# A decode step of attention with a gate: the last heads' output as columns, turned into 16 rows of 32

## The chip, the cores and the metric

The kernel runs on one core of a Trainium2 chip. Its time is device microseconds of one execution. The core has five engines that run side by side: TensorE (PE; the loading of its weights is shown as PEld), VectorE (DVE), ScalarE (ACT), GpSimd (POOL) and SyncE (SP), which here only issues DMAs. Data lie in HBM, in SBUF (128 partitions) and in PSUM, where TensorE writes its products. Engines wait for one another and for DMAs through semaphores.

## What is computed

One token x (512 numbers) is normalised to xn. Attention runs over the last 4096 positions of a cache of 32 heads with 128 numbers a head, and its result is multiplied by wo. A small MLP on xn gives a gate g, and the output is x + s * g.

```python
xn = _layernorm(x)
q = (xn @ wq)                       # 32 heads of 128
scores = q . k[:, last 4096, :] * 128**-0.5
o = softmax(scores) . v[:, last 4096, :]
s = o.reshape(4096) @ wo            # 4096 x 512
x1 = xn + hs                        # hs is made of shifted h: with one token all of it is zero
g = silu(x1 + gelu(layernorm(x1) @ w3) @ w4)
out = x + s * g                     # 512 numbers, bf16
```

K and V of the window are 32 MB each; with the weights the kernel reads 78.84 MB.

## The kernel before

**Groups.** The heads are taken in 8 groups of G = 4. One K tile or V tile (4 MB) holds a group: the 128 partitions are 4 heads by 32 blocks of 128 positions. The loop runs over s = 0 to 9: in turn s it loads K of group s and V of group h = s - 2 (LAG = 2), makes the scores of group s, the softmax of group s - 1, and the V products of group h. There are three K buffers and two V buffers; the V buffers lie where the front's weights (the pool `wts`) lay. All large loads are issued on SP's queue through `load`, in program order.

**Scores.** Of a group's 128 columns of K, `k_vector` has VectorE multiply some (`nd`: 76, 80 or 64) with q (L343) and sum the products (L345), in four parts a group. The others are turned by TensorE (`k_turn`, L361), copied to SBUF by ScalarE (L364) and multiplied by q on TensorE (`k_scores`, L372). `sm_own`, `sm_max`, `sm_turn`, `sm_exp`, `sm_den` and `sm_rden` are the softmax.

**V.** `v_wide` (L449) multiplies p with V, four columns at once, into four groups of rows of `ov`; ScalarE copies that, `v_turn` (L466) turns it, `v_add` (L471) sums it. In the last group V comes in four pieces (columns 0 to 64, 96, 112, 128); the last two pieces go through `v_part` (L482), whose weights are 128x128 of V and which multiplies four columns of p. `v_out` adds the two results (`both`, L494) and scales them (`o`, L497).

**Output product.** The first 28 heads are multiplied with wo in blocks of 16, 8 and 4 heads (`ox_spread`, `ox_pick`, `y_wide`) into four rows of 512 (`yr_ps`), copied to `y_sum` (L668). The last four heads (`y_head`) use four rows of wo_rows, of which the last (head 31) is loaded by itself, as the last load. `rows_add` (L150) is the helper that the change removes: it takes one column as weights (one column of the array) and multiplies it with a 128x512 matrix in four pieces of 128, so that the result lies as four rows of 128 on the partitions 0, 32, 64 and 96:

```python
for j in range(KC):
    nc.tensor.matmul(ps[32 * j:32 * j + 1, :], lhsT=col, rhs=w[0:k, j * P:(j + 1) * P], ...)
```

`y_ps` is opened with zeros by `rows_open`, gets the rows of `y_sum` (with the indicator `ind` as the column) and those of the last four heads, and is then multiplied by `g_row` (L680), added to `x_row` (L682) and stored from the four partitions.

**The front.** x is loaded as 16 rows of 32 (`x_in`) and turned into a column form for the normalisation. For the end it is also opened into the row form (`r_slot`, `r_row`, `r_up`, `r_in`, `xr_ps`, `x_row`, `xn_row`). The MLP's last sums come as rows `hr` (L295), which `rows_add` adds up into `h2_ps`; `bv` (L300) adds `xn_row`, and `g_row` is its Silu (L302), for which ScalarE loads a table of functions first.

**Order.** Before the loop, a scheduler of the language orders each engine's instructions. In the loop TensorE, VectorE and ScalarE keep the order of the text (`manual_schedule`); what belongs to the front and is not done by then is threaded in by the scheduler. Each engine runs its list in order, so an instruction that waits holds up all behind it.

Of the kernel before, what the change touches and what calls it, by code (L numbers as in the profile page):

```python
# [8 lines left out]
P = 128  # L9
BF16 = mybir.dt.bfloat16  # L10
# [16 lines left out]
def kernel(  # L27
# [43 lines left out]
    small.tile([P, 208], BF16, name="pad")  # L71
    wts_guard = tc.tile_pool(name="wts", bufs=1)
    wts = wts_guard.__enter__()

# [71 lines left out]
    def rows_open(ps):  # L146
        nc.tensor.matmul(ps[:], lhsT=zero_bf[:], rhs=ident_bf[:], start=True, stop=False,
                         skip_group_check=True)

    def rows_add(ps, col, w, last):  # L150
        k = col.shape[0]
        for j in range(KC):
            nc.tensor.matmul(ps[32 * j:32 * j + 1, :], lhsT=col, rhs=w[0:k, j * P:(j + 1) * P],  # L153
                             start=False, stop=last, skip_group_check=True)

    def ln_stats(src_f, tag):
        ps = ps_misc.tile([P, KC], FP32, tag="misc", name="ln_ps")
# [81 lines left out]
    for j in range(KC):  # L239
        for c in range(KC):  # L240
# [9 lines left out]
    nc.vector.tensor_reduce(out=r_slot[:], in_=ident_bf[0:XR, 0:XR].rearrange("k (j a) -> k a j", a=KC), axis=AX.X, op=ALU.max)  # L250
    r_row = wts.tile([XR, KC], BF16, name="r_row")
    nc.vector.tensor_reduce(out=r_row[:], in_=ident_bf[0:XR, 0:XR].rearrange("k (j a) -> k j a", a=KC), axis=AX.X, op=ALU.max)
    r_up = wts.tile([XR, KC, PB], BF16, name="r_up")
    nc.vector.tensor_copy(out=r_up[:], in_=r_row[:].unsqueeze(2).to_broadcast([XR, KC, PB]))
# [3 lines left out]
    xr_ps = ps_misc.tile([P, P], FP32, tag="misc", name="xr_ps")  # L258
# [37 lines left out]
    h2_ps = ps_misc.tile([P, P], FP32, tag="misc", name="h2_ps")  # L296
# [14 lines left out]
    y_ps = ps_y.tile([P, P], FP32, name="y_ps")  # L311
    rows_open(y_ps)

# [119 lines left out]
    def wo_row(h):  # L433
        return wo_rows[:, h - h_part, :]
# [77 lines left out]
    def ox_pick(i, fill=0):  # L512
# [12 lines left out]
                                    op=ALU.add)  # L525
        ox_blk[i] = ox

    y_sum = small.tile([P, D], FP32, name="y_sum")

    yr = {}  # L530

# [27 lines left out]
    for s in range(NG + LAG):  # L559
# [22 lines left out]
        if s < NG:  # L582
            nb = len(batches(s))

            def keys(b0, b1):
                for b in range(b0, b1):
                    k_turn(s, kn, b)
                    if b > 0:
                        k_scores(s, b - 1)

            k_open(s)
            k_vector(s, kn, 0)
            keys(0, 2)
            if s == 7:
                v_turn(h - 1)
                v_add(h - 1)
                v_out(h - 1)
            elif s > 1:
                sm_den(s - 2)
                sm_rden(s - 2)  # L600
            elif s == 1:
                sm_max(0)
            k_vector(s, kn, 1)
            keys(2, 4)
            if s == 7:
                sm_den(h)
                sm_rden(h)
                keys(4, nb - 2)
                sm_turn(s - 1)
                keys(nb - 2, nb)  # L610
            else:
                if s > 0:
                    sm_turn(s - 1)
                keys(4, nb)
            k_scores(s, nb - 1)
            sm_own(s)
            if s == 7:
                k_vector(s, kn, 2)
                v_wide(h, v)
                sm_exp(s - 1)  # L620
                v_turn(h)
                y_open()
                k_vector(s, kn, 3)
                v_add(h)
                v_out(h)
                ox_spread(1)
                sm_max(s)
                continue
            if s > 0:
# [12 lines left out]
            if s == 6:  # L642
                ox_pick(0)
            if s > 0:
                sm_max(s)
        elif s == NG:
            ox_pick(1)
            sm_turn(NG - 1)
            sm_exp(NG - 1)
            y_wide(1, False)  # L650
            sm_den(NG - 2)
            sm_rden(NG - 2)
            y_wide(0, False)
            warm(3)
            v_wide(h, v)
            sm_den(NG - 1)
            sm_rden(NG - 1)
            v_turn(h)
            v_add(h)
            v_out(h)  # L660
            ox_spread(2)
        else:
            v_open(h)
            warm(2)
            v_wide(h, v, cuts[1], last=False)
# [12 lines left out]
    region.__exit__(None, None, None)  # L678
    y = small.tile([P, P], FP32, name="y")
    nc.vector.tensor_tensor(out=y[:], in0=y_ps[:], in1=g_row[:], op=ALU.mult)  # L680
    out_row = small.tile([P, P], BF16, name="out_row")
    nc.vector.tensor_tensor(out=out_row[:], in0=y[:], in1=x_row[:], op=ALU.add)  # L682
    load(out.rearrange("a b (j n) -> (a b j) n", j=KC), out_row[0:P:32, :])


# [28 lines left out]
```

## Time and profile before

| | |
|---|---|
| median of 3 runs | 192.71 us (192.57 to 192.85) |
| profiled execution | 192.51 us |
| its span | 190.7 us |
| VectorE busy | 154.9 us (81%) |
| TensorE busy | 119.6 us (63%), weight loads 74.9 us |
| ScalarE busy | 89.0 us (47%) |
| moved by DMA | 79.02 MB, mean 414 GB/s |
| mean granted TensorE clock | 0.689 of full |

The span is the time from the first instruction to the last that the profiler recorded in one execution. Busy time says how long an engine worked, not whether anything waited for it. In a row of groups or of the timeline stand the line of the kernel, the engine, the operation, `out<-in` by the names of the tiles, their shapes and the count. "Releaser" is what ended an idle time. The strips of digits show 40 equal slices of the span, about 4.8 us each.

### The profile page before, as it was taken

How to read it: one execution, taken by the hardware profiler on the slowest of the kernel's cores; microseconds unless marked ns; L12 is line 12 of the kernel's file. 1: busy time of each engine (PE TensorE's matmuls, PEld its weight loads, DVE VectorE, ACT ScalarE, POOL GpSimd, SP SyncE). 2: the span in 40 equal slices, each digit the busy share in tenths (PEclk: the TensorE clock that was granted, in tenths of full speed). 3: DMA queues.
4: the chain of work that ended last, by engine and by line, in shares of the span. 5: the costliest groups of instructions: out<-in, count | busy, mean ns of one | idle time of the engine just before them, and what ended most of it. 6: DMA issues, size and time to landing. Idle time of an engine off the chain costs nothing.

```text
span 190.7 us, 2819 instructions
## 1 busy us (share of the span) xinstructions
PE 119.6 (63%) x1143; PEld 74.9 (39%) x1143; DVE 154.9 (81%) x184; ACT 89.0 (47%) x191; POOL 2.2 (1%) x10
## 2 busy tenths in 40 slices
PE   2446834778656169436964684573878386769972
PEld 1331313566545154334344433440854075423331
DVE  4830169999999999999999999999999999990112
ACT  2000821978686066607382737362575148644120
POOL 2110000000000000000000000000000000000000
PEclk9999985555555555965585569558575559785897
DMA  5999999999999999999999999999999998999991
GB/s 214 448 404 435 455 402 431 440 440 433 436 435 440 440 440 436 426 433 440 423 412 405 440 436 416 457 440 433 436 440 442 426 419 378 464 426 416 414 380 43
DMA packets 4597, 79.02 MB, mean 414 GB/s; under 512 B 520, under 2 KB 1128, under 8 KB 1640
## 3 DMA queue, kind: packets, MB, share of 16 engines
q1 hardware_dynamic: 4408, 74.65, 91.5%
q10 hardware_dynamic: 176, 4.20, 5.1%
q8 instruction: 9, 0.15, 0.3%
q14 instruction: 4, 0.03, 0.0%
HBM read 78.84 MB, written 0.00 MB: 413 GB/s over the span
## 4 chain that ended last, share of the span: by engine, by line
DVE 71%; DMA 20%; PE 3%; SPq 2%; issue 1%; ACT 1%; DVEq 0%; ACTq 0%
DVE S L345 43%; DVE prod L343 22%; DMA kv<-in_A_k_cache_dram 12%; DMA kv<-in_A_v_cache_dram 8%; SPq L76 2%; PE ov L449 2%; DVE m L388 1%; DVE S L386 1%; ACT kt L364 1%; DVE mx L396 1%; DVE md L398 0%; DVE oT L471 0%; DVE hr L295 0%; DVE ox L524 0%; PE y_ps L153 0%
## 5 line engine op out<-in xcount | busy, mean ns | idle before, releaser
L345 DVE TENSOR_REDUCE S<-prod 128x20 f32<-128x2560 bf16 (+2 forms) x32 | 87.6, 2736 | 1.1
L364 ACT COPY kt<-pt 128x1024 bf16<-128x1024 bf16 (+1 forms) x51 | 49.7, 1004 | 43.9 <-PE pt L361 42.7
L361 PE MATMUL pt<-ident_f,kv 128*128 128x128 f32 x202 | 46.1, 381 | 7.4 <-DMA kv<-in_A_k_cache_dram 7.4
L343 DVE TENSOR_TENSOR prod<-kv,q_bc 128x2560 bf16<-128x2560 bf16 (+2 forms) x32 | 46.1, 1442 | 3.3 <-DMA kv<-in_A_k_cache_dram 3.1
L361 PEld LDWEIGHTS pt<-ident_f,kv 128*128 128x128 f32 x202 | 34.0, 199 | 11.3 <-DMA kv<-in_A_k_cache_dram 8.7
L372 PE MATMUL sT<-q_pair,kt 128*128 128x8 bf16 x404 | 19.0, 170 | 16.2 <-ACT kt L364 16.0
L372 PEld LDWEIGHTS <-kt 128*128 128x128 bf16 x404 | 16.2, 105 | 26.5 <-ACT kt L364 25.5
L449 PE MATMUL ov<-kv,pT 128*16 128x512 bf16 x248 | 24.4, 561 | 0.4 <-DMA kv<-in_A_v_cache_dram 0.4
L394 PE MATMUL mt_ps<-ident_f,m 128*1 128x128 f32 x8 | 2.9, 360 | 18.4 <-DVE rden L421 17.5
L455 ACT COPY ov_sb<-ov 128x512 f32<-128x512 f32 x8 | 4.7, 585 | 20.3 <-PE ov L449 20.3
L410 ACT ACTIVATE pT<-S,mb 128x128 bf16<-128x128 f32 x32 | 14.0, 574 | 0.2
L449 PEld LDWEIGHTS <-pT 128*16 128x16 bf16 x248 | 7.1, 117 | 14.5 <-issue 13.7
L381 ACT ACTIVATE own<-sT,par 128x48 f32<-128x48 f32 (+2 forms) x32 | 7.5, 352 | 3.7 <-PE sT L372 3.7
L466 PE MATMUL ot_ps<-ident_f,ov_sb 128*128 128x128 f32 x32 | 7.5, 378 | 1.8 <-ACT mb L406 1.5
L410 ACT ACTIVATION_READ_ACCUMULATOR pT<-S,mb 128x1 f32 x32 | 8.3, 260 | 0.0
L218 ACT CAST q_row<-qr_ps 128x512 bf16<-128x512 f32 x1 | 0.6, 585 | 16.5 <-PE qr_ps L216 16.5
L394 PEld LDWEIGHTS mt_ps<-ident_f,m 128*1 128x1 f32 x8 | 0.6, 80 | 19.1 <-DVE rden L421 17.9
L403 PE MATMUL mb_ps<-md,par_t 5*128 5x4 f32 x16 | 4.3, 336 | 5.9 <-DVE md L398 5.9
L421 DVE RECIPROCAL rden<-den_ps 128x4 f32<-128x4 f32 x8 | 1.4, 175 | 7.6 <-PE den_ps L416 7.6
L219 DVE CAST q_row<-qr_ps 128x512 bf16<-128x512 f32 x1 | 0.7, 692 | 7.4 <-PE qr_ps L216 7.4
L403 PEld LDWEIGHTS mb_ps<-md,par_t 5*128 5x128 f32 x16 | 3.8, 293 | 6.9 <-PE sT L372 5.6
L466 PEld LDWEIGHTS ot_ps<-ident_f,ov_sb 128*128 128x128 f32 x32 | 4.8, 188 | 2.4 <-ACT mb L406 1.9
(136 smaller groups left out, 85.3 us busy)
## 6 DMA issues: line engine op xcount, KB each, us to landing
kv<-in_A_k_cache_dram SPq DMA_DIRECT2D x7, 4096.0 KB, 30.7
kv<-in_A_v_cache_dram SPq DMA_DIRECT2D x7, 4096.0 KB, 29.6
wq_sb<-in_A_wq_dram ACTq DMA_DIRECT2D x1, 4096.0 KB, 17.3
kv<-in_A_k_cache_dram SPq DMA_DIRECT2D x2, 2048.0 KB, 23.0
wo<-in_A_wo_dram SPq DMA_DIRECT2D x1, 2048.0 KB, 28.8
kv<-in_A_v_cache_dram SPq DMA_DIRECT2D x1, 2048.0 KB, 12.9
w_sb<-in_B_w_dram SPq DMA_DIRECT2D x1, 1376.0 KB, 12.5
w_sb<-in_B_w_dram SPq DMA_DIRECT2D x1, 1280.0 KB, 19.0
```

The source lines that it names most:

```text
L76: return tc.keep_in_program_order(nc.sync.dma_start(out=dst, in_=src))
L343: nc.vector.tensor_tensor(out=prod[:, 0:m, :], in0=kn[:, rows, :], in1=q_bc[:, g:g + 1, :].to_broadcast([P, m, Dh]), op=ALU.mult)
L345: nc.vector.tensor_reduce(out=st[g]["S"][:, rows], in_=prod[:, 0:m, :], axis=AX.X, op=ALU.add)
L361: nc.tensor.transpose(pt[:, i, :], kn[:, c:c + 2, :].rearrange("p c d -> p (c d)").bitcast(FP32), ident_f[:])
L364: nc.scalar.copy(out=kts[b][:, 0:n, :], in_=pt[:, 0:n, :].bitcast(BF16))
L372: nc.tensor.matmul(st[g]["sT"][:, c:c + 2, :].rearrange("p c a -> p (c a)"), lhsT=kt[:, i, l::2], rhs=q_pair[:, g, l, :], start=(l == 0), ...
L381: nc.scalar.mul(s["own"][:, 0:m, a], s["sT"][:, 0:m, a], par[:, a:a + 1])
L403: nc.tensor.matmul(mb_ps[:], lhsT=par_t[:].rearrange("k b a -> k (b a)"), rhs=md[:], start=True, stop=True)
L410: nc.scalar.activation(out=s["pT"][:, :, a], in_=s["S"][:], func=ACT.Exp, scale=scale, bias=mb[:, a:a + 1], accum_out=s["sum"][:, a:a + 1])
L449: nc.tensor.matmul(ov[r:r + 4 * G], lhsT=s["pT"][:, c:c + 4, :].rearrange("p i a -> p (i a)"), rhs=v[:, c:c + 4, :], start=(i < 4), stop=( ...
L455: nc.scalar.copy(out=s["ov_sb"][:], in_=ov[:])
L466: nc.tensor.transpose(ot_ps[:, step * j:step * j + P], s["ov_sb"][:, j, :], ident_f[:])
```

## The change

The last heads' output is made as columns. `y_head` takes 128x128 of wo_rows as weights and multiplies the one column o with it, so that number j * 128 + d of the output lies at partition d, column j, of `y_cols` (part of the tile `yz_ps`). At the end `t_last` multiplies these by `g_own`, the gate with a mask: 16 columns (j, q), in which a partition has its value only where q is its block of 32 partitions. One product with `fold`, which brings together the partitions that are equal modulo 32, makes of it `z_rows`: 16 rows of 32 on the partitions 0 to 15. `x_in` is added and the 16 rows are stored.

The four rows of `y_sum` go the same way: `y_turn` turns them with four transposes, sums the four (`y_first`) and multiplies them by `g_own` (`t_first`); `z_add` adds them into `z_rows` while the last V pieces are still coming. In the front x's normalised form is made as a column (`xn_col`), and the MLP's rows `hr` are summed with `hr` as the weights (128x128, f32) and `ind` as the column, so that `bv` and the gate (`g_col`) are 128x4. Some pads in the pools of tiles are new or of another size.

```diff
-    r_up = wts.tile([XR, KC, PB], BF16, name="r_up")
-    nc.vector.tensor_copy(out=r_up[:], ...)
...
-    nc.tensor.matmul(xr_ps[:], lhsT=r_up[:].rearrange("k j b -> k (j b)"), rhs=r_in[:].rearrange("k a n -> k (a n)"),
-                     start=True, stop=True)
-    x_row = small.tile([P, P], BF16, name="x_row")
-    nc.vector.tensor_copy(out=x_row[:], in_=xr_ps[:])
-    xn_row = small.tile([P, P], FP32, name="xn_row")
-    nc.vector.tensor_scalar(out=xn_row[:], in0=x_row[:], scalar1=negmean[:], scalar2=rstd[:],
+    nc.tensor.matmul(xt_ps[:], lhsT=r_in[:].rearrange("k a n -> k (a n)"), rhs=r_row[:], start=True, stop=True)
+    xn_col = small.tile([P, KC], FP32, name="xn_col")
+    nc.vector.tensor_scalar(out=xn_col[:], in0=xt_ps[:], scalar1=negmean[:], scalar2=rstd[:],
...
-    rows_open(h2_ps)
-    rows_add(h2_ps, ind, hr, True)
-    bv = small.tile([P, P], FP32, name="bv")
-    nc.vector.tensor_tensor(out=bv[:], in0=xn_row[:], in1=h2_ps[:], op=ALU.add)
-    g_row = small.tile([P, P], FP32, name="g_row")
-    nc.scalar.activation(out=g_row[:], in_=bv[:], func=ACT.Silu)
+    for j in range(KC):
+        nc.tensor.matmul(h2_ps[:, j:j + 1], lhsT=hr[:, j * P:(j + 1) * P], rhs=ind[:], start=True, stop=True)
+    bv = small.tile([P, KC], FP32, name="bv")
+    nc.vector.tensor_tensor(out=bv[:], in0=xn_col[:], in1=h2_ps[:], op=ALU.add)
+    g_col = small.tile([P, KC], FP32, name="g_col")
+    nc.scalar.activation(out=g_col[:], in_=bv[:], func=ACT.Silu)
...
+    g_own = small.tile([P, KC, NQ], FP32, name="g_own")
+    nc.vector.tensor_tensor(out=g_own[:], in0=g_col[:].unsqueeze(2).to_broadcast([P, KC, NQ]),
+                            in1=masks[4][2][:].unsqueeze(1).to_broadcast([P, KC, NQ]), op=ALU.mult)
+    fold_f = const.tile([P, XC], FP32, name="fold_f")
+    nc.vector.tensor_reduce(out=fold_f[:], in_=ident_f[:].rearrange("d (i t) -> d t i", t=XC), axis=AX.X, op=ALU.max)
...
-    y_ps = ps_y.tile([P, P], FP32, name="y_ps")
-    rows_open(y_ps)
+    yz_ps = ps_y.tile([P, KC + XC], FP32, name="yz_ps")
...
+    y_cols, z_rows = yz_ps[:, 0:KC], yz_ps[0:XR, KC:KC + XC]
...
     def y_head(h):
-        rows_add(y_ps, o_blk[3][:, h - h_part:h - h_part + 1], wo_row(h), h == H - 1)
+        for j in range(KC):
+            nc.tensor.matmul(y_cols[:, j:j + 1], lhsT=wo_row(h)[:, j * P:(j + 1) * P],
+                             rhs=o_blk[3][:, h - h_part:h - h_part + 1], start=False, stop=(h == H - 1),
+                             skip_group_check=True)
+
+    def y_turn():
+        yt_ps = ps_misc.tile([P, KC, P], FP32, tag="misc", name="yt_ps")
+        for j in range(KC):
+            nc.tensor.transpose(yt_ps[:, j, :], y_sum[:, j * P:(j + 1) * P], ident_f[:])
+        y_first = small.tile([P, KC], FP32, name="y_first")
+        nc.vector.tensor_reduce(out=y_first[:], in_=yt_ps[:].rearrange("p j (i m) -> p j i m", m=32)[:, :, :, 0],
+                                axis=AX.X, op=ALU.add)
+        t_first = small.tile([P, KC, NQ], FP32, name="t_first")
+        nc.vector.tensor_tensor(out=t_first[:], in0=y_first[:].unsqueeze(2).to_broadcast([P, KC, NQ]), in1=g_own[:],
+                                op=ALU.mult)
+        return t_first
+
+    def z_add(t, fold, last):
+        nc.tensor.matmul(z_rows, lhsT=t[:].rearrange("p j q -> p (j q)"), rhs=fold[:], start=False, stop=last,
+                         skip_group_check=True)
...
-            rows_add(y_ps, ind, y_sum, False)
+            t_first = y_turn()
             v_part(h, v, cuts[2], cuts[3])
             v_turn(h)
+            z_add(t_first, fold_f, False)
...
-    y = small.tile([P, P], FP32, name="y")
-    nc.vector.tensor_tensor(out=y[:], in0=y_ps[:], in1=g_row[:], op=ALU.mult)
-    out_row = small.tile([P, P], BF16, name="out_row")
-    nc.vector.tensor_tensor(out=out_row[:], in0=y[:], in1=x_row[:], op=ALU.add)
-    load(out.rearrange("a b (j n) -> (a b j) n", j=KC), out_row[0:P:32, :])
+    t_last = small.tile([P, KC, NQ], BF16, name="t_last")
+    nc.vector.tensor_tensor(out=t_last[:], in0=y_cols.unsqueeze(2).to_broadcast([P, KC, NQ]), in1=g_own[:], op=ALU.mult)
+    z_add(t_last, fold_bf, True)
+    out_sb = small.tile([XR, XC], BF16, name="out_sb")
+    nc.vector.tensor_tensor(out=out_sb[:], in0=z_rows, in1=x_in[:], op=ALU.add)
+    load(out.rearrange("a b (r n) -> (a b r) n", r=XR), out_sb[:])
```

More of the change, by code (lines that the diff above doesn't have):

```diff
@@ L70 @@
     sm_pool = ctx.enter_context(tc.tile_pool(name="sm", bufs=3))
-    small.tile([P, 208], BF16, name="pad")
+    small.tile([P, 240], BF16, name="pad")
     wts_guard = tc.tile_pool(name="wts", bufs=1)
@@ L144, in zeros @@
                          start=True, stop=False, skip_group_check=True)
[L146 to L154, printed above, removed]
     def ln_stats(src_f, tag):
@@ L252 @@
     nc.vector.tensor_reduce(out=r_row[:], in_=ident_bf[0:XR, 0:XR].rearrange("k (j a) -> k j a", a=KC), axis=AX.X, op=ALU.max)
-    r_up = wts.tile([XR, KC, PB], BF16, name="r_up")
-    nc.vector.tensor_copy(out=r_up[:], in_=r_row[:].unsqueeze(2).to_broadcast([XR, KC, PB]))
     r_in = wts.tile([XR, KC, XC], BF16, name="r_in")
@@ L257 @@
                             in1=r_slot[:].unsqueeze(2).to_broadcast([XR, KC, XC]), op=ALU.mult)
-    xr_ps = ps_misc.tile([P, P], FP32, tag="misc", name="xr_ps")
-    nc.tensor.matmul(xr_ps[:], lhsT=r_up[:].rearrange("k j b -> k (j b)"), rhs=r_in[:].rearrange("k a n -> k (a n)"),
-                     start=True, stop=True)
-    x_row = small.tile([P, P], BF16, name="x_row")
-    nc.vector.tensor_copy(out=x_row[:], in_=xr_ps[:])
-    xn_row = small.tile([P, P], FP32, name="xn_row")
-    nc.vector.tensor_scalar(out=xn_row[:], in0=x_row[:], scalar1=negmean[:], scalar2=rstd[:],
+    xt_ps = ps_misc.tile([P, KC], FP32, tag="misc", name="xt_ps")
+    nc.tensor.matmul(xt_ps[:], lhsT=r_in[:].rearrange("k a n -> k (a n)"), rhs=r_row[:], start=True, stop=True)
+    xn_col = small.tile([P, KC], FP32, name="xn_col")
+    nc.vector.tensor_scalar(out=xn_col[:], in0=xt_ps[:], scalar1=negmean[:], scalar2=rstd[:],
                             op0=ALU.add, op1=ALU.mult)
@@ L295 @@
     nc.vector.tensor_copy(out=hr[:], in_=hr_ps[:].rearrange("p j n -> p (j n)"))
-    h2_ps = ps_misc.tile([P, P], FP32, tag="misc", name="h2_ps")
-    rows_open(h2_ps)
-    rows_add(h2_ps, ind, hr, True)
-    bv = small.tile([P, P], FP32, name="bv")
-    nc.vector.tensor_tensor(out=bv[:], in0=xn_row[:], in1=h2_ps[:], op=ALU.add)
-    g_row = small.tile([P, P], FP32, name="g_row")
-    nc.scalar.activation(out=g_row[:], in_=bv[:], func=ACT.Silu)
+    h2_ps = ps_misc.tile([P, KC], FP32, tag="misc", name="h2_ps")
+    for j in range(KC):
[4 more added lines that the diff above has]
+    nc.scalar.activation(out=g_col[:], in_=bv[:], func=ACT.Silu)
     make_masks(16)
@@ L307 @@
     make_masks(4)
-    y_ps = ps_y.tile([P, P], FP32, name="y_ps")
-    rows_open(y_ps)
+    NQ = P // XC
+    g_own = small.tile([P, KC, NQ], FP32, name="g_own")
[3 more added lines that the diff above has]
+    nc.vector.tensor_reduce(out=fold_f[:], in_=ident_f[:].rearrange("d (i t) -> d t i", t=XC), axis=AX.X, op=ALU.max)
+    fold_bf = const.tile([P, XC], BF16, name="fold_bf")
+    nc.vector.tensor_copy(out=fold_bf[:], in_=fold_f[:])
+    yz_ps = ps_y.tile([P, KC + XC], FP32, name="yz_ps")
+    nc.tensor.matmul(yz_ps[:], lhsT=zero_bf[:], rhs=zero_bf[:, 0:KC + XC], start=True, stop=False,
+                     skip_group_check=True)
+    y_cols, z_rows = yz_ps[:, 0:KC], yz_ps[0:XR, KC:KC + XC]
     par = const.tile([P, G], FP32, name="par")
@@ L526, in ox_pick @@
         ox_blk[i] = ox
+    small.tile([P, 48], BF16, name="pad_rows")
     y_sum = small.tile([P, D], FP32, name="y_sum")
+    small.tile([P, 32], BF16, name="pad_result")
     yr = {}
@@ L550, in y_head @@
     def y_head(h):
-        rows_add(y_ps, o_blk[3][:, h - h_part:h - h_part + 1], wo_row(h), h == H - 1)
+        for j in range(KC):
[15 more added lines that the diff above has]
+        nc.tensor.matmul(z_rows, lhsT=t[:].rearrange("p j q -> p (j q)"), rhs=fold[:], start=False, stop=last,
+                         skip_group_check=True)
     NG = H // G
```

## The prediction

> **What bounds the kernel now.** I read the page first: the strip of busy tenths, then the chain that ended last.
>
> ```profile
> span 190.7 us, 2819 instructions
> ...
> DVE  4830169999999999999999999999999999990112
> ...
> DMA  5999999999999999999999999999999998999991
> ...
> DVE 71%; DMA 20%; PE 3%; SPq 2%; issue 1%; ACT 1%; DVEq 0%; ACTq 0%
> ...
> kv<-in_A_v_cache_dram SPq DMA_DIRECT2D x1, 2048.0 KB, 12.9
> ```
>
> The chain names VectorE for 71%, but the DMA strip is at nine tenths or more from the second slice to the last but one. VectorE only decides when buffers come free, and those loads wait in a queue anyway: the first piece of the last V group, 2 MB, lands 12.9 us after its issue, and at the page's 414 GB/s it needs 5.1 us of the stream, so some 8 us of earlier transfers stood ahead of it. A load issued under 8 us later lands at the same time. The stream is the bound, and what follows it is the tail.
>
> The tail is in the timeline at the end of the span (start, duration, instruction):
>
> ```profile
> 185.96 0.56 PE L482 MATMUL oP<-pT,kv 128*128 128x4 bf16 x16 [0.18 <-DMA kv<-in_A_v_cache_dram]
> ...
> 187.02 0.49 PE L153 MATMUL y_ps<-wo_rows,o 128*1 128x128 bf16 x11
> 187.29 0.09 PEld L153 LDWEIGHTS <-o 128*1 128x1 bf16 x3
> 187.57 0.29 DVE L680 TENSOR_TENSOR y<-y_ps,g_row 128x128 f32<-128x128 f32 x1 [0.65 <-PE y_ps L153]
> 187.90 0.29 DVE L682 TENSOR_TENSOR out_row<-y,x_row 128x128 bf16<-128x128 f32 x1
> 188.21 0.66 SPq L76 DMA_DIRECT2D out_dram<-out_row  x1
> ```
>
> The chain shows the sixteen L153 products as released by o (done at 186.92). The finer rows say otherwise: twelve go at once, and the last head's group begins at 187.29. The last load, row block 31 of wo_rows, was issued at 171.3 and lands after 15.9 us, that is at 187.2. So the path is: stream ends (187.2), last head's four products, two VectorE operations, store. Whatever ends before 187.2 costs nothing. I also asked for VectorE's waits between 26 and 160 us:
>
> ```profile
> DVE prod L343 <- DMA kv<-in_A_k_cache_dram: 3.1, 1, 3.1
> ```
>
> One wait, before its first product at 25.65. After that VectorE is never idle, so a delay put into it near 32 us arrives whole at 160.
>
> **The change part by part.** *Last heads' products.* Before, four products into four partition rows start within some 0.01 us, their one-column weights being loaded already. After, each of sixteen weight loads brings 128x128 of wo_rows and multiplies one column, the shape of L482: sixteen pairs in 0.56, that is 0.025 a pair and some 0.18 for the last. Twelve pairs from 186.97 take 0.30, to 187.27, still under the landing of block 31 (seen at 187.29). The last four then end at 187.29 + 0.26 = 187.55 where they ended at 187.52: +0.03. If the cover were gone, the twelve would cost 0.2.
>
> *The end of the arithmetic.* Before: from 187.52 to the store's issue at 188.21, 0.69. After: handover 0.05, t_last as pick (128x16, 0.175), handover 0.05, the turning product as ox_ps (L516, 0.18), handover 0.05, out_sb as pick or x_pick (0.175 to 0.19), handover 0.03: 0.71. The two smaller VectorE operations save 0.23 and the product with its handovers takes 0.25: +0.02.
>
> *The store.* Sixteen rows of 64 B take the place of four of 256 B. The trace has the old store (issue 0.66, its end seen by SP at 189.9, 1.7 after its start) and one DMA of the new shape, the load of x: 16 rows, issue 0.41, landing 2.8 after its start, in a crowd of other loads. Issue: between 0.41 and 0.66; I take 0.48, the last wo_rows issue, nearest in time and queue: -0.18. After the issue the store of four took 1.0 and the load of sixteen 2.4, so the change lies between about -0.2 (it lands as before or a little faster with smaller rows) and +1.4. The old store's packets all fall between 189.4 and 189.6; those of the load are spread over some 0.6 us (17 of its 32, completions included, in 2.5 to 2.95, 15 in 2.95 to 3.3). Nearest is the old store (same queue, same direction, no crowd), so I take the lower part, +0.3: store +0.12 in all, ends -0.45 and +1.4.
>
> The Trainium skill (DMA: Bandwidth & Descriptors, section "Why a DMA increments its semaphore by 16 and not by 1") says that a DMA is spread over the largest number of engines up to 16 that divides its outer size, and that the issuer itself writes the increments of the unused ones. By that rule the store goes from 4 engines to 16 and waits for the slowest of them, while its issue gets shorter; the longer issue of the old store (0.66 against 0.41 to 0.48) agrees, and what the sixteen cost at the landing no run here shows.
>
> *g and x at the front.* Removed: r_up, x_row, xn_row, the opening product. Added: fold_f and fold_bf near 9 us. The pads keep the tiles' places, and SP's order of issues is the same: nothing. All of the setup stands where VectorE idles from 10 to 25 us waiting for K; free, with 15 us of cover. But h2 comes later. Before, its products ran 30.64 to 31.24 while VectorE was in the product that ended at 31.73, so bv did not wait. After, each of four f32 products loads 128x128 weights in two passes; L158, the same form, takes 0.56 for two passes, 0.33 more for each further pair: 0.56 + 3 x 0.33 = 1.55 from 30.45, to 32.0. bv starts near 32.05 instead of 31.64, and is shorter by 0.1: +0.3. Then g_own, a new VectorE operation, stands between the second reduce and the third product and waits for ScalarE's Silu. ScalarE's order in the built program has that Silu behind one kt copy (about 33.55), its table load 1.28 and itself 0.2 to 0.3: done near 35.1. The reduce is done at 34.85, so VectorE waits 0.3, g_own takes 0.17, and the third product starts near 35.3 instead of 34.56: 0.75 late. Behind it stands all of VectorE's chain. For the stream that is nothing (8 us of backlog); if the backlog were gone it would cost 0.75. It does reach TensorE, which waits for VectorE once in every group: the last group's first products (L449 at 181.12) would start up to 0.75 later.
>
> *What is put into the last stage.* y_turn has four f32 transposes where there were eight one-row products, two VectorE operations, and z_add. VectorE was idle there for 3.1 before L471, so its two cost nothing. On TensorE, from L449's start: 1.64 to the y products, 0.43 and 0.58 until y_sum is copied, 0.05, four transposes like L466's 0.49, sixteen pairs 0.40, four transposes 0.49, z_add 0.2: 4.3. That is 185.4 if L449 starts at 181.12, and the last V piece lands at 185.91: 0.5 to spare. A start 0.75 late would leave it 0.25 over. The clock softens it: granted 0.50 in 174.3 to 177.7 and 1.00 in 177.8 to 181.2, so 0.75 of half-clock work takes some 0.4 at full clock, inside the margin. I put 0.05 here, ends 0 and +0.3.
>
> The sum: 0.03 + 0.02 + 0.12 + 0.05 = +0.22. The profiled execution took 192.51 (span 190.7 and 1.8 around it), 0.20 under the median of the runs; 192.51 becomes 192.7, and the median 192.71 becomes 192.9.
>
> **The rivals.** *The store lands late* (slower). All sixteen packets must be confirmed; if they spread as those of the x load, +0.6 for the spread, and up to +1.4. For it: the only 16-row DMA of the trace. Against: that one ran in a crowd, and read. With +0.6 the sum is +0.52: 193.2; it decides from a landing 0.5 above the old one. The skill's sixteen engines, above, are this rival's mechanism.
>
> *TensorE comes late to the last pieces* (slower). The 0.75 of VectorE is not softened, or the clock is still at half when the last group starts. Transposes then start 0.21 apart, as L361's at 31.8, so each 0.49 becomes 0.9, and the L449 products slow down too: up to 2 us over. For it: the margin is only 0.5, and twelve pairs have no cover left. Against: the clock was full from 177.8 to 187.9. Likely price 0.5 on top of the sum: 193.4; it decides from a start of L449 0.5 late. The Trainium skill (TensorE: Matmul & The Clock Gate, section "What's actually happening") has the clock decided in free-running windows of 3.4 us; the trace's change between 177.7 and 177.8 fits, but what the phase is in another run, no run here shows.
>
> *The store is faster* (the other side). The four-row form costs its issue 0.25 more than 0.41, and smaller rows land 0.35 sooner: -0.6 on the store instead of +0.12, sum -0.5: 192.2. It decides from a store of under 1.2 in all. For it: the issues at the start, of 16 to 128 rows, took 0.39 to 0.63. Against: no DMA of the trace lands in under 2.8 after its start except the old store's 1.7.
>
> **How the numbers follow.** The forecast 192.9 (own range 192.4 to 193.1) gets 0.47; late store 0.2; late TensorE 0.17; faster store 0.16. What a measurement here can tell from no change is about 0.2%, 0.39 us: 192.32 to 193.10. So slower 0.2 + 0.17 = 0.37, same 0.47, faster 0.16. The range reaches to both slower cases' likely prices and to the edge of the faster one: 192.35 to 193.5.
>
> **What would show it.** In the profile after: h2's products end near 32.0, VectorE waits before bv and before g_own, and the third L343-like product starts near 35.3; the last V pieces land as before and the last wo_rows block near 187.2; the turning product adds some 0.25 between two VectorE operations of under 0.2; the store's issue is under 0.55. I am wrong if the last V products wait for TensorE instead of a DMA, if the last load lands elsewhere than 187.2, or if the store's end comes more than 0.5 away from 1.7 after its start.

## The result

The changed kernel takes 193.98 us (median of six executions, 193.44 to 194.46) where the kernel before takes 192.69 (192.57 to 192.85): a ratio of 1.0066, 95% interval 1.0049 to 1.0083. It is slower by 1.29, and above the whole range of the forecast. Its profiled execution, 193.44, is the quickest of the six; against the 192.51 of the profile before it is 0.93 longer. What the profile shows explains these 0.93; the median moved by more.

### The profile page after: what moved, and what is told of

Read it like the earlier page. It is cut to its first block, busy times and chain, and to the rows that moved or that the text cites. A ratio compares the mean times of both kernels' runs of the same rounds, so it can differ in the third digit from the quotient of the medians.

```text
span 191.6 us, 2818 instructions
## 1 busy us (share of the span) xinstructions
PE 123.0 (64%) x1141; PEld 78.5 (41%) x1141; DVE 155.0 (81%) x187; ACT 89.1 (46%) x191; POOL 2.2 (1%) x10
## 4 chain that ended last, share of the span: by engine, by line
DVE 70%; PE 14%; DMA 9%; ACT 4%; issue 1%; ACTq 0%; DVEq 0%
DVE S L340 42%; DVE prod L338 21%; DMA wq_sb<-in_A_wq_dram 9%; PE ov L444 3%; PE yr_ps L543 2%; PE qr_ps L206 2%; PE pt L356 1%; DVE m L383 1%; DVE S L381 1%; PE h_ps L283 1%; PE wm L532 1%; PE ot_ps L461 1%; ACT kt L359 1%; DVE mx L391 1%; ACT L287 1%
## 5 line engine op out<-in xcount | busy, mean ns | idle before, releaser
L356 PE MATMUL pt<-ident_f,kv 128*128 128x128 f32 x202 | 47.3, 388 | 5.0 <-DMA kv<-in_A_k_cache_dram 5.0
L356 PEld LDWEIGHTS pt<-ident_f,kv 128*128 128x128 f32 x202 | 35.0, 204 | 8.3 <-DMA kv<-in_A_k_cache_dram 6.1
L444 PE MATMUL ov<-kv,pT 128*16 128x512 bf16 x248 | 23.9, 551 | 0.0
L389 PE MATMUL mt_ps<-ident_f,m 128*1 128x128 f32 x8 | 3.0, 372 | 21.4 <-DVE rden L416 19.5
L444 PEld LDWEIGHTS <-pT 128*16 128x16 bf16 x248 | 7.0, 116 | 13.9 <-issue 13.0
L389 PEld LDWEIGHTS mt_ps<-ident_f,m 128*1 128x1 f32 x8 | 0.6, 79 | 22.1 <-DVE rden L416 20.1
## 6 DMA issues: line engine op xcount, KB each, us to landing
kv<-in_A_v_cache_dram SPq DMA_DIRECT2D x1, 2048.0 KB, 11.3
```

Source lines behind the costliest of these rows:

```text
L356: nc.tensor.transpose(pt[:, i, :], kn[:, c:c + 2, :].rearrange("p c d -> p (c d)").bitcast(FP32), ident_f[:])
L444: nc.tensor.matmul(ov[r:r + 4 * G], lhsT=s["pT"][:, c:c + 4, :].rearrange("p i a -> p (i a)"), rhs=v[:, c:c + 4, :], start=(i < 4), stop=( ...
```

## The profile after

The page of the changed kernel: VectorE's strip still has no gap, the DMA strip is full until its last two slices, and the chain that ended last has a new name in second place.

```profile
span 191.6 us, 2818 instructions
...
DVE  4730168999999999999999999999999999982021
...
PEclk9999695555555555855695558557655858585798
DMA  6999999999999999999999998999999999999980
...
DVE 70%; PE 14%; DMA 9%; ACT 4%; issue 1%; ACTq 0%; DVEq 0%
...
kv<-in_A_v_cache_dram SPq DMA_DIRECT2D x1, 2048.0 KB, 11.3
```

TensorE had 3% of the chain before and has 14% now. The first piece of the last V group is issued later (11.3 us to its landing instead of 12.9) and lands at the same time, 181.2 against 181.0: the stream did not move, as forecast. The tail, from the timeline (start, duration, instruction):

```profile
182.91 1.04 PE L444 MATMUL ov<-kv,pT 128*16 128x512 bf16 x16
...
187.09 0.23 PE L566 MATMUL yz_ps<-fold_f,t_first 128*16 128x32 f32 x2
...
187.25 0.56 PE L477 MATMUL oP<-pT,kv 128*128 128x4 bf16 x16
...
188.26 0.54 PE L549 MATMUL yz_ps<-o,wo_rows 128*128 128x1 bf16 x16 [0.45 <-DVE o L492]
...
188.84 0.17 DVE L697 TENSOR_TENSOR t_last<-yz_ps,g_own 128x16 bf16<-128x16 f32 x1 [0.63 <-PE yz_ps L549]
...
189.06 0.18 PE L566 MATMUL yz_ps<-fold_bf,t_last 128*16 128x32 bf16 x1 [0.27 <-DVE t_last L697]
189.29 0.18 DVE L700 TENSOR_TENSOR out_sb<-yz_ps,x_in 16x32 bf16<-16x32 f32 x1 [0.28 <-PE yz_ps L566]
189.49 0.35 SPq L76 DMA_DIRECT2D out_dram<-out_sb  x1
```

The last V products no longer carry a wait for a DMA. Their piece landed at 186.1, and they began at 187.25, when TensorE had come to them. That splits the 0.93 in three:

| | before | after | difference |
|---|---|---|---|
| start of the last V products | 185.96 | 187.25 | +1.29 |
| from there to the store's issue | 2.25 | 2.24 | -0.01 |
| from the store's issue to the end of the span | 2.51 | 2.16 | -0.35 |

The store became faster; TensorE lost more than three times that. (That +1.29 is also the difference of the two medians is chance.) The last block of wo_rows landed at 187.4, near the 187.2 forecast, but nothing waited for it any more: the last heads' products start at 188.26, behind o. The last group's first products (L444; before L449) begin at 182.91, 1.79 after the 181.12 of before. Where that starts is in VectorE's waits between 26 and 165 us:

```profile
DVE prod L338 <- ACT q_row L216: 2.1, 1, 2.1
DVE bv L285 <- PE h_ps L283: 0.6, 1, 0.6
DVE mx L391 <- PE mt_ps L389: 0.5, 1, 0.5
DVE g_own L295 <- ACT g_col L287: 0.3, 1, 0.3
```

The second and the fourth line are new; before, the third was 0.4. The timeline shows what stands behind them:

```profile
30.41 1.86 PE L283 MATMUL h_ps<-ind,hr 128*128 128x1 f32 x8 [3.82 <-DVE hr L280]
...
32.31 0.16 DVE L285 TENSOR_TENSOR bv<-xn_col,h_ps 128x4 f32<-128x4 f32 x1 [0.63 <-PE h_ps L283]
...
35.16 0.20 ACT L287 ACTIVATE g_col<-bv 128x4 f32<-128x4 f32 x1
...
35.40 0.18 DVE L295 TENSOR_TENSOR g_own<-g_col,mh 128x16 f32<-128x16 f32 x1 [0.33 <-ACT g_col L287]
...
35.49 1.42 DVE L338 TENSOR_TENSOR prod<-kv,q_bc 128x2432 bf16<-128x2432 bf16 x1
```

The third product starts at 35.49 instead of 34.56, 0.93 late, and 125 us later VectorE is still late by the same amount (a product of the last K group starts at 159.11 instead of 158.17). Between there and 182.91 TensorE loses another 0.86. The granted clock shows where. The first fence is the kernel before, the second the changed one, each in its own steps of 3.4 us (window, busy times by engine, granted clock, DMA):

```profile
160.70:164.10 3.40, 2.10 (x33) 1.67 (x33) 2.97 (x6) 2.40 (x4) 0.00 (x0) 1.00 0.94 396
164.10:167.50 3.40, 2.87 (x36) 1.16 (x40) 3.33 (x3) 1.47 (x5) 0.00 (x0) 0.50 1.18 502
167.50:170.90 3.40, 1.98 (x20) 0.96 (x12) 3.30 (x7) 2.38 (x10) 0.00 (x0) 1.00 1.07 463
```

```profile
159.10:162.50 3.40, 1.87 (x26) 1.48 (x26) 3.37 (x3) 2.53 (x3) 0.00 (x0) 1.00 0.90 376
162.50:165.90 3.40, 2.74 (x25) 2.19 (x25) 2.87 (x6) 1.66 (x2) 0.00 (x0) 0.50 1.16 487
165.90:169.30 3.40, 2.98 (x36) 1.27 (x40) 3.33 (x3) 1.36 (x5) 0.00 (x0) 0.50 0.96 414
169.30:172.80 3.50, 1.94 (x20) 0.88 (x8) 2.76 (x7) 2.38 (x10) 0.00 (x0) 0.99 1.02 440
```

Both kernels fall to half after a window in which TensorE was busy 55 to 62% of the time (1.87 and 2.10 of 3.4). Before, one window at half follows, busy for 84%, and the clock is full again. After, the first window at half is busy for 81% and a second one at half follows. Over 157 to 181 us the mean granted clock is 0.78 before and 0.67 after. The busy share of a window doesn't settle by itself what follows it: in the profile of before_near (below) a full window busy 59% (2.02 of 3.4, from 166.5) is followed by another full one, and a half-clock window that is busy throughout (from 156.2) by another at half.

## The experiments

Two theories were tested first. A: VectorE's two new waits near 32 us are the cause, and the store and the last stage as such are not. B: what was put into the last stage is the cause, and VectorE's delay is lost in the backlog of loads. Each kernel was timed beside the kernel before on the same chip.

**The gate's operations moved (late_gate).** `bv` and the Silu go behind the second reduce, `g_own` to turn 8; everything else is the changed kernel.

```diff
-    nc.vector.tensor_tensor(out=bv[:], in0=xn_col[:], in1=h2_ps[:], op=ALU.add)
-    nc.scalar.activation(out=g_col[:], in_=bv[:], func=ACT.Silu)
-    nc.vector.tensor_tensor(out=g_own[:], ...)
...
             k_vector(s, kn, 1)
+            if s == 0:
+                nc.vector.tensor_tensor(out=bv[:], ...); nc.scalar.activation(out=g_col[:], ...)
...
             y_wide(0, False)
+            nc.vector.tensor_tensor(out=g_own[:], ...)
             warm(3)
```

> The changed kernel with two VectorE operations and the Silu moved in the order: bv and g_col stand behind the second reduce (where h2 has long been done), g_own in the last stage, where VectorE is idle. Theory A (VectorE's waits in the front, 0.93 us of them, make TensorE late at the last V pieces): VectorE is back within 0.2 of the kernel before, the last V products wait for their DMA again (start near 186.0), and with the shorter store the time is 192.2 to 192.7. Theory B (the work put into the last stage, y_turn, the 128x128 weights and the turning product, costs the time by itself): the time stays at 193.5 to 194.3.

Measured: 192.55 (192.25 to 193.17) beside 192.78, ratio 0.9989 (0.9981 to 0.9998). The third product is at 34.70, and the last V products start at 186.35, as soon as their DMA has landed (186.31; in this profile the V pieces land 0.40 later than in that of before, so the start is not the 186.0 expected). From its timeline:

```profile
186.35 0.56 PE L473 MATMUL oP<-pT,kv 128*128 128x4 bf16 x16
...
188.60 0.35 SPq L76 DMA_DIRECT2D out_dram<-out_sb  x1
```

A holds: with the front's order mended, the whole new tail is a small gain.

**The kernel before with a busy VectorE (before_busy).** Two operations that write `y_sum` (which is written again before its use) stand between the second reduce and the third product.

```diff
+            if s == 0:
+                for e0, e1 in ((0, 512), (0, 256)):
+                    nc.vector.tensor_tensor(out=y_sum[:, e0:e1], in0=ones_f[:, 0:1].to_broadcast([P, e1 - e0]), ...)
             k_vector(s, kn, 1)
```

> The kernel before with two VectorE operations of about 0.9 us together (they fill y_sum with ones, which is overwritten later) between the second reduce and the third product of the first group. Theory A: VectorE is 0.9 late from there to its end, TensorE 0.9 to 1.8 late at the last group, and the time is 193.0 to 194.0. Theory B: the load stream covers it, 192.6 to 192.8.

Measured: 193.69 (193.57 to 195.27) beside 192.78, ratio 1.0077 (1.0048 to 1.0105). The old tail loses 0.9 and more from a late VectorE too, so B falls as the main cause. It is not without a part: in this profile the old tail goes from its first products (184.59) to its last V products (188.53) in 3.94 with no wait for a DMA, the new one in 4.34 (182.91 to 187.25), both at full clock. What was put into the last stage has thus taken 0.40 of a margin of 0.90 (185.96 less 181.12 less 3.94). Its executions lie in two groups, four at 193.57 to 193.69 and three at 195.06 to 195.27. The profiled one is of the second: third product at 35.72 (1.16 late; 0.2 of it because the first product starts later), the last group's first products 3.47 late, and the granted clock at half throughout, as its row of 157 to 181 us in the busy times by window says (the 0.50 behind the busy times of PE, PEld, DVE, ACT and POOL):

```profile
157.00:181.00 24.00, 20.30 (x165) 10.96 (x167) 15.48 (x22) 11.37 (x29) 0.00 (x0) 0.50 0.99 424
```

**Only g_own moved (late_own).** The diff is the last part of late_gate's alone.

> The changed kernel with g_own alone moved to the last stage; bv still waits for h2. Theory A: VectorE is 0.5 late instead of 0.93, and the time lies between: 192.5 to 193.5. Theory B: as the changed kernel, 193.5 to 194.3.

Measured: 193.12 (192.41 to 194.0), ratio 1.0018 (1.0003 to 1.0033), between the two. The wait of bv stays (0.6) and the third product is at 35.35, 0.79 late where 0.5 was expected (the first product starts at 25.9 instead of 25.65). The profiled execution (193.80) has a clock of 0.59 in 157 to 181 and its first products at 183.28, later than the changed kernel's own profile although its VectorE is earlier. So the delay does not set TensorE's lateness by itself.

**Four rows instead of sixteen (late_gate_4rows).** On late_gate: the turning product gives four rows of 128 on partitions 0 to 3, and x is loaded once more in that form.

```diff
+    x_four = small.tile([KC, P], BF16, name="x_four")
+    nc.scalar.dma_start(out=x_four[:], in_=A_x.rearrange("a b (r n) -> (a b r) n", r=KC))
...
-    load(out.rearrange("a b (r n) -> (a b r) n", r=XR), out_sb[:])
+    load(out.rearrange("a b (r n) -> (a b r) n", r=KC), out_sb[:])
```

> late_gate, but the turning product multiplies with the identity, so that the output lies as 4 rows of 128 on partitions 0 to 3 and is stored as 4 rows of 256 B (x is loaded once more in that shape). If the shorter store of the changed kernel (issue 0.35, landing 1.3 after its start, against 0.66 and 1.7) is due to the 16 rows, the store is back at 0.66 and 1.7, and with the 0.1 that the larger last operations take the time is 0.4 to 0.5 above late_gate. If it is due to something else (neighbouring partitions, the moment), the store keeps 0.35 and 1.3 and the time is 0.1 above late_gate.

Measured: 193.36 (193.22 to 193.43), ratio 1.0029 (1.0018 to 1.004). The store's issue is 0.33, in the timeline:

```profile
186.94 0.56 PE L474 MATMUL oP<-pT,kv 128*128 128x4 bf16 x16
...
189.43 0.33 SPq L76 DMA_DIRECT2D out_dram<-out_sb  x1
```

So the short issue does not come from sixteen rows. The kernel is slower for two other reasons: its last V products, behind their DMA, start 0.59 later than in late_gate (the stream had an added load at the start, which may be why; that was not separated), and from there to the store took 2.49 instead of 2.25, with products into 128 columns instead of 32.

**The store alone (before_near).** One slice of the kernel before. Rows 1 to 3 of out_row are not the result, so this kernel does not give the result; it shows only what the store costs.

```diff
-    load(out.rearrange("a b (j n) -> (a b j) n", j=KC), out_row[0:P:32, :])
+    load(out.rearrange("a b (j n) -> (a b j) n", j=KC), out_row[0:KC, :])
```

> Only the partitions that the kernel before stores from are changed: 0, 1, 2, 3 instead of 0, 32, 64, 96. It stores other rows than the result's (rows 1 to 3 of out_row are not the answer), still four of 256 B. Theory "neighbouring partitions make the store cheap" (four rows of 256 B from neighbouring partitions had an issue of 0.33 in the run with 4 rows, 0.66 from every 32nd): issue 0.33 to 0.36, time 0.3 to 0.4 below the kernel before, 192.3 to 192.5. Theory "more and smaller rows make it cheap, and the 4-row run had another reason": issue 0.66 as before, time within 0.15 of the kernel before.

Measured: 192.32 (192.1 to 192.52) beside 192.72, ratio 0.9977 (0.9968 to 0.9986). The page's span and the timeline's last line:

```profile
span 190.3 us, 2819 instructions
```

and

```profile
188.31 0.34 SPq L76 DMA_DIRECT2D out_dram<-out_row  x1
```

Nothing but the partitions was changed: the issue falls from 0.66 to 0.34, and from its start to the end of the span it is 2.0 instead of 2.5. The sixteen rows of the change need 2.16. Whether it is the step between the partitions or which partitions they are was not separated.

**The clock held up (after_warm).** TensorE gets six products of zeros where it waits for VectorE, four before the product mt_ps (L389) of group 6 (a wait of 1.34 in the changed kernel, in the window above after which the clock falls) and two in turn 8.

```diff
                 keys(4, nb - 2)
+                warm(4)
                 sm_turn(s - 1)
...
             ox_pick(1)
+            warm(2)
             sm_turn(NG - 1)
```

> The changed kernel with six products of zeros by zeros added, which nothing reads: four of 512 columns where TensorE waits 1.34 us for VectorE's maxima in the changed kernel (161.45 to 162.79, just before the clock falls to half) and two where it waits 0.57 (172.25 to 172.83). VectorE stays 0.93 late. Theory "the clock adds to the delay": with these waits filled the clock stays full between 162 and 171, the last group's first products start 0.9 to 1.2 later than before's 181.12 instead of 1.79, and the time is 193.2 to 193.5 with less spread than 193.44 to 194.46. Rival "the half-clock windows don't hang on those waits": the clock is at half in as many windows as in the changed kernel, the start is 1.8 or more late, and the time is 193.9 to 194.6.

Measured: 192.72 (192.39 to 193.78) beside 192.72, ratio 1.0015 (0.9999 to 1.0031). The profiled execution (192.44) has VectorE as late as ever, and yet TensorE is in time, by its timeline and its row of 157 to 181 us:

```profile
35.47 1.42 DVE L338 TENSOR_TENSOR prod<-kv,q_bc 128x2432 bf16<-128x2432 bf16 x1
...
181.56 1.04 PE L444 MATMUL ov<-kv,pT 128*16 128x512 bf16 x16
```

and

```profile
157.00:181.00 24.00, 17.95 (x197) 9.42 (x196) 15.32 (x23) 11.66 (x30) 0.00 (x0) 0.86 1.00 424
```

With a clock of 0.86, a third product 0.91 late leaves the first products only 0.44 late, inside the margin (and the V piece they need landed at 181.31, 0.3 later than before). More work on TensorE made the kernel faster: by 1.1 to 1.3 in the medians (193.82 and 193.98 without it), by 0.8 to 1.0 in the means (192.95 against 193.73 and 193.98) and by 0.3 to 0.5% in the ratios (1.0047 and 1.0066; the interval is clear of the first one's and just touches the second's). Both theories missed, as the time is lower than either said. That the clock is the way by which the filling helps fits the profile, in which it stays full from 157.0 to 170.6, but the profile does not prove it: it is of a quick execution, and its clock was full from 157.0, before the first added product at 161.27, where that of the profile after was full only from 159.1. The expected lower spread did not come: seven executions are at 192.39 to 192.81, five at 193.28 to 193.78, and the first seven have a mean clock over the whole execution of 0.682 to 0.715, the five of 0.673 to 0.694. The filling helps in some executions and not in others.

**The same filling on late_gate (late_gate_warm).**

> The same six products added to the kernel with the gate's operations moved (192.55 in its runs), whose TensorE waits at the two places are 0.53 and 0.57. There the last V products wait for their DMA, so TensorE's time before them is worth nothing while it stays inside its margin. Theory "the stream is the bound again": 192.4 to 192.7, no difference that can be measured. Rival "some of its executions still lose to the clock" (its runs reach up to 193.17): the median falls by 0.1 to 0.2 and the upper end comes under 192.8. If the added products do not fit into the waits, they delay the scores of the last group by up to 0.9 and the time rises to 193 or more.

Measured: 192.88 (192.38 to 193.91), ratio 1.0013 (0.9996 to 1.003). Both theories missed: the executions split into six at 192.38 to 192.59 and six at 193.18 to 193.91, where late_gate without the filling had none over 193.17. The third case named, added products that don't fit and a time of 193 or more, has the times of the second six. Where VectorE is in time, the added products are a risk. The profiled execution is of the first six (192.38), so what the other six lose is not shown.

**The changed kernel once more (after_again).**

> The changed kernel once more, beside the next two and beside the kernel before on the same chip, for its spread: its six runs lay between 193.44 and 194.46. If the clock's windows fall as they like from one execution to the next, the times spread over 193.0 to 194.5 and the profiled execution shows the half-clock windows elsewhere; the last group's first products start 0.9 to 2.0 after before's 181.12. If they are tied to the program, the windows lie as in the first profile (half in 162.5 to 169.3 and 172.8 to 179.6) and the times within 0.3 of 194.0.

Measured: 193.82 (192.69 to 194.79), ratio 1.0047 (1.0028 to 1.0067). The windows of the clock are not tied to the program: this profile (194.07) has half clock all the way from 153 to 170, where the first had a full window from 159.1 to 162.5. The spread and the lateness are even larger than the 193.0 to 194.5 and the 0.9 to 2.0 expected: its first products start at 183.55 and its last V products at 187.89, 1.93 after before's. With the store's 0.35 taken off that is about the 1.56 by which it exceeds 192.51. Its row of 157 to 181 us:

```profile
157.00:181.00 24.00, 20.30 (x179) 11.08 (x179) 15.49 (x22) 11.36 (x29) 0.00 (x0) 0.58 0.99 423
```

**The last stage relieved (turn_late).** The transposes of y_sum and what follows them go behind the last V products.

```diff
-            t_first = y_turn()
             v_part(h, v, cuts[2], cuts[3])
             v_turn(h)
-            z_add(t_first, fold_f, False)
             v_add(h)
             v_part(h, v, cuts[3], CP)
+            yt_ps = y_turn()            # only the transposes
             v_out(h)
+            t_first = y_fold(yt_ps)     # y_first and t_first
             for r in range(H - G, H):
                 y_head(r)
+            z_add(t_first, fold_f, False)
```

> The changed kernel with only the last stage's order changed: the four transposes of y_sum go behind the last V products, their two VectorE operations behind o, and their product into z behind the last heads' products. The front is that of the changed kernel, so VectorE is 0.93 late and TensorE 1 to 2 late. In the changed kernel the way from the last group's first products to its last V products takes 4.34 (182.91 to 187.25); without the transposes, the product and their waits it takes 3.0 to 3.4. Theory "the delay costs what exceeds the last stage's margin": the last V products start at 186.1 to 186.3, as their DMA allows, up to a start of the first products at 182.9; the added work lies beside o (0.4 to 0.5) and the wait for the last load, at most 0.3 of it is seen; time 192.4 to 193.0. Rival "the late front costs by itself, whatever the margin": 193.6 to 194.2.

Measured: 193.55 (192.67 to 194.56), ratio 1.0032 (1.0015 to 1.0049); the interval overlaps that of after_again. In the profiled execution (193.55) the first products start at 183.36 and the last V products at 187.06, in the timeline:

```profile
183.36 1.04 PE L444 MATMUL ov<-kv,pT 128*16 128x512 bf16 x16
...
187.06 0.55 PE L477 MATMUL oP<-pT,kv 128*128 128x4 bf16 x16
...
189.60 0.35 SPq L76 DMA_DIRECT2D out_dram<-out_sb  x1
```

The way is 3.70 instead of 4.34, not the 3.0 to 3.4 expected, and 0.30 of the gain is given back behind it (2.54 to the store instead of 2.24). The start was past 182.9, the point up to which the expectation held. The median lies between the ranges of the two theories, and the run tells little against either: the margin grew by 0.64 to 1.14, and this execution is 2.24 late.

**Both orders (both_late).** turn_late's last stage on late_gate.

> The same order of the last stage in the kernel with the gate's operations moved (192.55, ratio 0.9989 to the kernel before, its runs up to 193.17). Theory "margin": no execution comes late to the last pieces, so the upper end falls under 192.8; the median is that of the moved gate or up to 0.3 above it, for what of the transposes' work is seen behind the last V products: 192.4 to 192.8. Rival "the work behind the last V products is on the path": the four transposes (0.64), two VectorE operations (0.4) and the product (0.25) are not covered by o and the wait for the last load: 193.0 to 193.4.

Measured: 192.50 (192.4 to 192.77) beside 192.78, ratio 0.9988 (0.9979 to 0.9996). Its last V products begin at 186.01 behind their DMA. As expected by the margin, no execution has the time of one that came late: the upper end is 0.4 under late_gate's. It has the lowest median of the kernels that give the result, 0.28 under the kernel before; by its ratio it can't be told from late_gate (0.9989).

The profiled executions side by side (the third product started at 34.56 before, the first products of the last group at 181.12):

| kernel | third product late | mean clock, 157 to 181 us | first products late | profiled time |
|---|---|---|---|---|
| both_late | 0.10 | 0.80 | none (wait for their DMA) | 192.50 |
| late_gate | 0.14 | 0.78 | 0.35 (wait for their DMA, landed 181.43) | 192.56 |
| after_warm | 0.91 | 0.86 | 0.44 | 192.44 |
| after | 0.93 | 0.67 | 1.79 | 193.44 |
| turn_late | 1.15 | 0.61 | 2.24 | 193.55 |
| late_own | 0.79 | 0.59 | 2.16 | 193.80 |
| after_again | 1.17 | 0.58 | 2.43 | 194.07 |
| before_busy | 1.16 | 0.50 | 3.47 | 195.22 |

Each row is one execution. The times follow the clock far better than VectorE's delay. Without the filling, every profile with a late VectorE (five) has a clock of 0.50 to 0.67, and those with VectorE in time (before, late_gate, both_late, before_near) 0.78 to 0.80. That a late VectorE makes TensorE's waits fall so that windows are less filled is what the two fences of the profile after suggest; it was not forced by an experiment, before_near's two windows above show that the filling of a window is not all of it, and why the same kernel's executions differ by up to 2.1 us is open beyond that.

## Why the prediction was wrong, and where it was right

**The step that failed** is the last one of the sum, "What is put into the last stage": 0.05, ends 0 and 0.3. It measured 1.29. What failed in it is the softening of the delay by the clock: the delay grew before it reached the last group. Its parts:

- The margin was right. It put the way from the first products to the last V products at 4.3 and the margin at 0.5. The way is 4.34 (182.91 to 187.25; again 183.55 to 187.89 in after_again), the margin 0.50 (185.96 less 181.12 less 4.34). What is over 0.50 costs all of itself: 1.79 - 0.50 = 1.29, of which VectorE's 0.93 alone would have made 0.43. The other 0.86 is what TensorE lost on the way to its last group, where the prediction expected the delay to shrink.
- VectorE's delay was put a little too small: 0.75 against 0.93. The order of it, with waits at bv and g_own, was right, and the wait at g_own was the 0.3 forecast. The missing part is h2's products: 1.86 instead of 1.55. The 0.33 a product came from L158, which ran while the clock strip stood at nine; near 31 us it stands at 5, and L361's row of that stretch, 0.21 a pass, stands further down in the prediction (for the transposes) and would have given 8 x 0.21 and the end of the last, near 1.9.
- "The clock softens it" was wrong in sign. The text took the granted clock of the profile before (full from 177.8) as fixed and let the late work run in it. In the changed kernel the clock is another one (half in 162.5 to 169.3 and 172.8 to 179.6; elsewhere again in after_again). From VectorE's lateness to that of the first products the loss grew by 0.86 in the first profile (clock 0.67), by 1.26 in after_again (0.58) and by 2.31 in before_busy (0.50), and it shrank by 0.47 in after_warm (0.86). That the clock makes this difference is argued from these pairs; why it fell as it did stays open.

The rival "TensorE comes late to the last pieces" names the path and its turning point (a start 0.5 late), at 0.17 and a price of 0.5 on the sum. It has the time lost in the last group at half clock; there the clock was full (from 179.6), and the loss lay before it. The price stood far under the rival's own "up to 2 us over", and "up to 2" is what the executions show.

**The store** was mis-sized: +0.12 was forecast, about -0.35 measured. The issue was taken at 0.48 and is 0.35, and the landing was taken 0.3 later and is not later at all (from the issue's end to the end of the span 1.81 against 1.85), so nearly all of the gain is the issue. The rival "the store is faster" had the direction, but not the reason or the size: it has the four-row form cost the issue more and smaller rows land sooner, and it was to decide from a store of under 1.2; the store took 1.3 to its landing, and before_near shows the short issue with the same four rows. The two rivals were priced as if only one could happen; a late TensorE and a faster store both came, and -0.35 hides part of +1.29. The Trainium skill (DMA: Bandwidth & Descriptors, section "Why a DMA increments its semaphore by 16 and not by 1") spreads a DMA over the largest number up to 16 that divides its outer size, and has the issuer write the unused increments. That this lengthens the issue was the prediction's own conclusion, from the old store's 0.66. The run of before_near decides otherwise: four rows, by that rule four engines as before, have an issue of 0.34 once they lie on neighbouring partitions.

**Right:** the stream's end (V pieces landed within 0.2 of before; in late_gate, late_own and after_again some 0.4 later), the setup of g and x at no cost in itself, the end of the arithmetic (0.71 forecast; from the products' end near 188.80 to 189.49 it is 0.69), the sixteen last products with their weights of 128x128 (0.54 instead of 0.55), and the turning product as 0.25 between two operations of under 0.2 (0.27 waited). The signs that the text named for being wrong are the ones that came: the last V products wait for TensorE instead of a DMA.

## What to carry to other kernels

Where an engine has no idle time between a point and the end, a wait of half a microsecond put into its list arrives whole at the far end; put a small operation that waits for another engine behind the long one that can cover it. A granted clock read in one profile is no constant of the next: two profiles of the changed kernel have 0.67 and 0.58 in the same 24 us. So price a delay on a half-idle TensorE with both clocks and take the spread over executions as part of the answer. Before rearranging the end of a kernel for its store, try the same store from neighbouring partitions: that alone was worth 0.40 here, more than both_late's whole gain of 0.28.

## What the runs showed that was not expected

- The issue of a 1 KB store takes 0.66 from every 32nd partition and 0.33 to 0.35 from neighbouring ones, with four rows as with sixteen.
- The median went down by 1.1 to 1.3 us (the mean by 0.8 to 1.0) when six products that nothing reads were added to the TensorE work of the changed kernel; added to late_gate they widened its spread.
- The granted clock fell to half after windows in which TensorE was busy 55 and 62%, and it came back after one busy 84 to 88% and not after one of 81%. No share decides alone: in before_near it stayed full after a window busy 59% and at half after one busy throughout. The Trainium skill (TensorE: Matmul & The Clock Gate, section "What's actually happening") has the state set by free-running windows of 3.4 us, which agrees with the steps here and with their different places in two profiles of one kernel; it gives an idle window as what takes the clock down, and here windows over half busy were enough.
